# Intermediate rows in DRAM 256 bytes further apart, and stores of z in two transfers by partition halves

## The chip, the core and the metric

The kernel runs on one core of one Trainium2 chip. The metric is the device time of one execution in microseconds, the median over runs. A core has TensorE (matrix products, results in PSUM), VectorE (DVE), ScalarE (ACT), GpSimd (POOL) and SyncE (SP), which here issues nearly all transfers between DRAM and the on-chip memory SBUF. SBUF has 128 partitions. 16 DMA engines carry out the transfers.

## The reference, cut to what matters

Two parts follow each other: a causal convolution over the whole sequence by FFT (8 batches, 5696 tokens, 128 channels), and a soft mixture of experts on the 45568 tokens that come out of it.

```python
L = 2 * S
Xf = np.fft.rfft(x, n=L, axis=1)
Hf = np.fft.rfft(h, n=L, axis=0)
y = np.fft.irfft(Xf * Hf[None, :, :], n=L, axis=1)[:, :S, :]
...
logits = x @ phi                      # x is now y, (45568, 128)
d = softmax over tokens of logits; slot_input = d.T @ x
slot_out = expert MLPs (relu) of slot_input
c = softmax over slots of logits
return c @ slot_out
```

(The lines of the second part are shortened here to what they compute.) All data are float32, and the change touches only how two intermediate results of the convolution lie in DRAM.

## The kernel before, in words

The transform of 2 x 5696 points is split into N1 = 90 by N2 = 64, so that each stage is a set of small matrix products. NP = 45 is half of N1, HP = 64 half of the 128 partitions, D = 128 the channels.

**Stage A** (stage_a, line 205) takes one chunk of four columns (CH = 4) of one batch, folded by GpSimd (L201), multiplies it with a table (L212), lets ScalarE copy the result to the tile fst (L214), and stores it in DRAM as the spectrum f of that batch (L218). Each store of f moves 45 partitions, four packets of 1 KB each; there are two for each call, one from partitions 6 to 50 and one from 82 to 126. Eight steps make a batch, with two calls a step. Batch 0 is the filter h.

**Stage B** works in units u: a batch has 12 units, one or two a step. load_g (line 230) loads for a unit 128 rows of 4 KB of f into the tile gt (L236; three buffers, two units ahead). stage_b1 multiplies (L250) and VectorE applies the filter's spectrum (L268, L277). stage_b2 (line 281) transforms back (L292), ScalarE copies to the tile zst (L297), and one transfer stores it in DRAM as z (L300): 128 partitions, up to four packets of 1 KB each.

**Stage C** works in pairs of chunks. load_pair (line 320) loads 90 rows of 16 KB of z into the tile zc in two transfers (L328), 64 rows to partitions 32 to 95 and 26 rows to partitions 0 to 25 (z_blocks). stage_c1 makes the convolution's output from it (L347), and the further C stages make logits, both softmaxes and the slots' inputs. After the last step a tail runs the experts and writes the output (L817 to L828).

The order is written out by hand in one loop over steps t (line 561), with stage A of batch g + 1, stage B of batch g and stage C of an earlier batch side by side. A load of zc needs rows of z from all 12 units of its batch, so the first load of each batch waits for that batch's last store. SyncE issues the transfers strictly in the order of the program. The tile framework gives the transfers eight completion semaphores in turn, and a transfer waits until the last one on its semaphore, the eighth before it, has landed, beside the waits for its own data and buffers.

The two DRAM tensors of the change are declared on lines 126 and 127. A row of f is 45 x 2 x 128 floats, 46080 bytes. z has for each of 45 q a block of 128 rows of 1 KB, 131072 bytes, and a load of zc reads it as 90 half blocks, 65536 bytes apart.

Of the kernel before, what the change touches and what calls it, by code (L numbers as in the profile page):

```python
# [10 lines left out]
F32 = mybir.dt.float32  # L11
# [6 lines left out]
def z_blocks(n):  # L18

    return [(0, 64, 32), (64, n - 64, 0)]  # L20
# [54 lines left out]
def kernel(  # L75
# [24 lines left out]
    nc = tc.nc  # L100
    P = 128
    B, S, D = x.shape
# [4 lines left out]
    N1, N2 = 90, 64  # L107
    R1, HALF, NP = S // N2, N2 // 2, N1 // 2
    CH = 4
# [6 lines left out]
    HP = P // 2  # L116
# [6 lines left out]
    t_s1, t_i1, t_w, t_v, t_turn = [  # L123
        nc.inline_tensor(t, f"tab_{n}").ap()
        for n, t in zip(("s1", "i1", "w", "v", "turn"), transform_tables(S, N1, N2, CH, X0, F0, F1))]
    fd = [nc.dram_tensor(f"f_{g}", (2, N2, NP, 2, D), F32, kind="Internal").ap() for g in range(B + 1)]
    zd = [nc.dram_tensor(f"z_{b}", (NP, 2 * N2, 2, D), F32, kind="Internal").ap() for b in range(B)]
    cd = nc.dram_tensor("c_t", (P, B * NQ, Q, 2, MH), F32, kind="Internal").ap()

    const = ctx.enter_context(tc.tile_pool(name="const", bufs=1))  # L130
# [37 lines left out]
    def bank():  # L168
        rings.append(rings.pop(0))
        return rings[-1].tile([P, 512], F32, name="bank", tag="bank")  # L170
# [34 lines left out]
    def stage_a(c, comp):  # L205
        g, j = divmod(c, NJ)
        src = folded.pop((c, comp))
        tab = (0, 1) if comp == 0 else (1, 2)
        st = apool.tile([P, CH, 2, D], F32, name="fst", tag="fst", bufs=5)
        for G in range(2):  # L210
            p = bank()
            nc.tensor.matmul(p[:, :], s1[:, tab[G], :],  # L212
                             src[:, :, :].rearrange("p n d -> p (n d)"), start=True, stop=True)
            nc.scalar.activation(st[:, :, G, :],  # L214
                                 p[:, :].rearrange("p (n d) -> p n d", d=D), AF.Copy)
        n0 = comp * HALF + CH * j
        for a, p in enumerate((F0, F1)):
            nc.sync.dma_start(  # L218
                out=fd[g][a, n0:n0 + CH, :, :, :].rearrange("n q c d -> q n (c d)"),
                in_=st[p:p + NP, :, :, :].rearrange("k n c d -> k n (c d)"))  # L220


# [2 lines left out]
    def parts(u):  # L225

        g, w = divmod(u, NW)
        return g, w, [(i, min(2, NP - 2 * i)) for i in range(2 * w, min(2 * w + 2, NU))]

    def load_g(u):  # L230
        if u >= (B + 1) * NW:
            return
        g, w, us = parts(u)
        n = sum(k for _, k in us)
        t_ = bpool.tile([P, 4, 2, D], F32, name="gt", tag="gt", bufs=3)
        nc.sync.dma_start(  # L236
            out=t_[:, 0:n, :, :].rearrange("p q c d -> p (q c d)"),
            in_=fd[g].rearrange("a r q c d -> (a r) (q c d)")[:, 8 * w * D:(8 * w + 2 * n) * D])
        gs[u] = t_

    def stage_b1(u, share):
# [39 lines left out]
    def stage_b2(u):  # L281
        g, w, us = parts(u)
        if g == 0:
            return
        m = len(us)
        y_ = prods.pop(u)
        bz = bps.tile([P, 2, 2, 2 * D], F32, name="bz", tag="bz")
        for o, (i, n) in enumerate(us):
            for q in range(n):
                r = slice(q * HP, (q + 1) * HP)  # L290
                for a in range(2):
                    nc.tensor.matmul(bz[a * HP:(a + 1) * HP, q, o, :], vt[r, i, a, :],  # L292
                                     y_[r, a * m + o, :, :].rearrange("p c d -> p (c d)"),
                                     start=True, stop=True)
        n = us[0][1]
        st = bpool.tile([P, 2, 2, 2 * D], F32, name="zst", tag="zst", bufs=3)
        nc.scalar.activation(st[:, 0:m, 0:n, :].rearrange("p o q x -> p q o x"),  # L297
                             bz[:, 0:n, 0:m, :], AF.Copy)
        k = m * n
        nc.sync.dma_start(  # L300
            out=zd[g - 1][4 * w:4 * w + k, :, :, :].rearrange("q r c d -> r q (c d)"),
            in_=st[:, :, :, :].rearrange("p o q x -> p (o q) x")[:, 0:k, :])

# [14 lines left out]
    def load_pair(T):  # L320
        if T >= NT:
            return
        b, j = divmod(T, NQ)
        t_ = zring.pop(0)
        zring.append(t_)
        w_ = 2 * 2 * CH * 2 * D
        for r, n, p in z_blocks(N1):
            nc.sync.dma_start(  # L328
                out=t_[p:p + n, :, :, :, :, :].rearrange("k h o n c d -> k (h o n c d)"),
                in_=zd[b].rearrange("q (a r) c d -> (q a) (r c d)",  # L330
                                    a=2)[r:r + n, j * w_:(j + 1) * w_])
        zs[T] = t_

    def stage_c1(T, between):
# [226 lines left out]
    for t in range(last_front + 1):  # L561
# [6 lines left out]
        def prefetch(last):  # L568
            nonlocal loaded
            while loaded < len(queue) and queue[loaded][0] <= last \  # L570
                    and queue[loaded][0] // NW * NJ + NJ <= t:
                load_g(queue[loaded][0])
                loaded += 1
# [3 lines left out]
        def slot_b(place=None):  # L577
            if place is not None and place not in turns:
                return
            fresh = bool(us)  # L580
            if fresh:
                u = us.pop(0)
                prefetch(u + AHEAD)
                stage_b1(u, t < LAG_C or t >= NA)
                wait_b2.append(u)
            if len(wait_b2) > fresh:
                stage_b2(wait_b2.pop(0))

        if t < NA:
            stage_a(t, 0)  # L590
            fold(t + 1, 0)
# [30 lines left out]
        if pair(-2) is not None:  # L622
            load_pair(pair(-2))
# [6 lines left out]
        if t < NA:  # L630
            stage_a(t, 1)
            fold(t + 1, 1)
# [11 lines left out]
        if NA < t <= NA + E:  # L644
# [13 lines left out]
                      in_=zring[0][gap, :, :, :, :, :].rearrange("k h o n c d -> k (h o n c d)"))  # L658
    zring.insert(0, zn)
    load_pair(V + 2)  # L660
    nc.sync.dma_start(out=w1s[:, E - 1, :], in_=moe_w1[E - 1])
    tail["cT"] = last.tile([P, B, R1, 2 * NJ], F32, name="cT")
# [10 lines left out]
    for q in range(Q):  # L673
        r = slice(q * NSL, (q + 1) * NSL)
        nc.gpsimd.tensor_copy(out=rep4[r, :, :],
                              in_=ident[r, r].unsqueeze(1).broadcast_to([NSL, Q, NSL]))
    load_pair(T + 2)
    landed = []

# [14 lines left out]
    for V in range(T, NT):  # L694
# [30 lines left out]
        else:  # L725
            for i in range(4 * (V - T - 1), min(4 * (V - T), E), 2):
                nc.sync.dma_start(
                    out=w2s[:, i:i + 2, :, :],
                    in_=moe_w2[i:i + 2].rearrange("e (p c) d -> p e c d", p=P))
# [6 lines left out]
    p = bank()  # L736
# [8 lines left out]
    p = bank()  # L745
# [12 lines left out]
    for g in range(EG):  # L758
        for f0 in range(0, F, FH):
            p = bank()  # L760
# [10 lines left out]
    for g in range(EG):  # L771
        for k0 in range(0, NFC, 4):
            p = bank()
            for k in range(4):
# [3 lines left out]
                out=hidT[:, g, k0:k0 + 4, :], in_=p[:, :].rearrange("p (k c) -> p k c", k=4))  # L778
# [9 lines left out]
    p = bank()  # L788
# [18 lines left out]
    for b in range(B):  # L807
        for w0 in range(0, NV, G4):
            n = min(G4, NV - w0)
# [10 lines left out]
            for q in range(Q):  # L820
# [8 lines left out]
                out=ov[b, t0:t0 + n * RW * N2, :].rearrange("(w p n) d -> p w (n d)", p=P, n=CH),  # L829
                in_=o_[:, 0:n, :, :].rearrange("p w q d -> p w (q d)"))  # L830
            if lone:
                nc.sync.dma_start(
                    out=ov[:, NV * RW * N2:, :].rearrange("b (j n) d -> b j (n d)", n=CH),
                    in_=o_[:, n, :, :].rearrange("p q d -> p (q d)"))
# [29 lines left out]
```

## Time and profile before

The time is 920.01 us, the median of three runs (918.54 to 926.59). The profiled run's span is 914.5 us.

| What | Value |
|---|---|
| VectorE busy | 645.8 us (71%) |
| ScalarE busy | 481.1 us (53%) |
| GpSimd busy | 405.2 us (44%) |
| Read from DRAM, written to it | 142.86 MB, 128.21 MB |
| Stores of f (L218) | 288 of 180 KB |
| Loads of gt (L236) | 99 of 512 KB, 9 of 128 KB |
| Stores of z (L300) | 88 of 512 KB, 8 of 128 KB |
| Loads of zc and its twin zd (L328) | 32 of 1024 KB, 32 of 416 KB |
| Granted TensorE clock | 0.945 in the mean |

"Busy" is the time in which an engine has an instruction running; the DMA share is the time of all packets over 16 engines' span. The chain is followed back from the last instruction, at each step to what released it, so its shares say on what the end depended. A wait is written as "who line <- by what": total us, how often, the longest. Mean values over the span hide that the stages differ: the loop fills up until about 190 us, runs evenly until 673 us, and then empties into the tail.

### The profile page before, as it was taken

How to read it: one execution, taken by the hardware profiler on the slowest of the kernel's cores; microseconds unless marked ns; L12 is line 12 of the kernel's file. 1: busy time of each engine (PE TensorE's matmuls, PEld its weight loads, DVE VectorE, ACT ScalarE, POOL GpSimd, SP SyncE). 2: the span in 40 equal slices, each digit the busy share in tenths (PEclk: the TensorE clock that was granted, in tenths of full speed). 3: DMA queues.
4: the chain of work that ended last, by engine and by line, in shares of the span. 5: the costliest groups of instructions: out<-in, count | busy, mean ns of one | idle time of the engine just before them, and what ended most of it. 6: DMA issues, size and time to landing. Idle time of an engine off the chain costs nothing.

```text
span 914.5 us, 19226 instructions
## 1 busy us (share of the span) xinstructions
PE 812.2 (89%) x7220; PEld 425.9 (47%) x7220; DVE 645.8 (71%) x928; ACT 481.1 (53%) x888; POOL 405.2 (44%) x385
## 2 busy tenths in 40 slices
PE   6968888799999999999999999999988776978893
PEld 2323344344454444544555445444444443345783
DVE  3058767667888878877888777868888885774552
ACT  4624445456556565655666565555654344474442
POOL 4624333245555555555555555555533432472000
PEclk9989999999999999999999999999999998788865
DMA  9999899999999999999999999989989998751798
GB/s 302 269 282 310 256 326 347 292 323 340 285 324 331 304 281 323 320 329 280 329 323 317 289 317 313 311 281 325 334 266 338 305 295 206 223 220 74 281 404 340
DMA packets 156550, 272.43 MB, mean 298 GB/s; under 512 B 11766, under 2 KB 114422, under 8 KB 153317
## 3 DMA queue, kind: packets, MB, share of 16 engines
q1 hardware_dynamic: 155883, 270.85, 91.7%
q8 instruction: 58, 0.95, 0.4%
q10 hardware_dynamic: 576, 0.36, 0.2%
q14 instruction: 33, 0.27, 0.1%
HBM read 142.86 MB, written 128.21 MB: 296 GB/s over the span
## 4 chain that ended last, share of the span: by engine, by line
PE 61%; DMA 27%; issue 4%; ACT 2%; DVE 2%; POOL 2%; SPq 1%; DVEq 0%; POOLq 0%; ACTq 0%
PE bank L212 19%; PE bank L347 10%; PE bt L250 9%; DMA zc<-z 8%; PE bz L292 7%; DMA gt<-f 6%; DMA out_dram<-o 4%; PE bank L375 3%; PE bank L460 3%; DMA zd<-z 3%; DMA z<-zst 2%; DMA f<-fst 2%; PE bank L384 2%; PE bank L436 2%; PE op L817 1%
## 5 line engine op out<-in xcount | busy, mean ns | idle before, releaser
L201 POOL TENSOR_TENSOR x<-xc 128x512 f32<-128x512 f32 x144 | 183.1, 1273 | 260.5 <-PE bank L212 156.9
L212 PE MATMUL bank<-x,s 128*128 128x512 f32 x576 | 273.9, 611 | 9.7 <-POOL x L201 9.6
L214 ACT ACTIVATE fst<-bank 128x512 f32<-128x512 f32 x288 | 171.8, 597 | 94.7 <-PE bank L212 88.3
L297 ACT ACTIVATE zst<-bz 128x1024 f32<-128x1024 f32 x96 | 93.2, 971 | 195.2 <-PE bz L292 191.5
L268 DVE TENSOR_TENSOR p<-bt,Hi 128x1024 f32<-128x1024 f32 x96 | 113.0, 1177 | 107.3 <-PE bt L250 107.1
L212 PEld LDWEIGHTS bank<-x,s 128*128 128x128 f32 x576 | 102.1, 192 | 126.9 <-issue 94.1
L250 PE MATMUL bt<-gt,wt 64*64 64x256 f32 x1620 | 117.4, 397 | 40.0 <-DMA gt<-f 19.8
L347 PE MATMUL bank<-zc,i 128*64 128x512 f32 x480 | 118.0, 614 | 8.5 <-DMA zc<-z 6.2
L277 DVE TENSOR_TENSOR yf<-bt,p 128x512 f32<-128x512 f32 x192 | 119.4, 663 | 3.3
L268 DVE TENSOR_TENSOR bt<-bt,Hr 128x1024 f32<-128x1024 f32 x96 | 113.0, 1178 | 0.0
L250 PEld LDWEIGHTS bt<-gt,wt 64*64 64x64 f32 x1620 | 55.9, 134 | 117.0 <-issue 61.7
L292 PE MATMUL bz<-yf,vt 64*64 64x256 f32 x1440 | 103.7, 386 | 0.0
L366 POOL TENSOR_TENSOR y<-y,op 128x512 f32<-128x512 f32 x64 | 77.4, 1209 | 11.8 <-DVE op L352 9.1
L292 PEld LDWEIGHTS bz<-yf,vt 64*64 64x64 f32 x1440 | 61.8, 136 | 21.1
L366 POOL TENSOR_TENSOR y<-y,om 128x512 f32<-128x512 f32 x54 | 64.0, 1185 | 2.1
L347 PEld LDWEIGHTS bank<-zc,i 128*64 128x64 f32 x480 | 30.9, 138 | 70.3 <-issue 47.4
L375 PE MATMUL bank<-ident,y 109*128 109x109 f32 x512 | 57.5, 268 | 0.7 <-DVE y L366 0.7
L375 PEld LDWEIGHTS bank<-ident,y 109*128 109x128 f32 x512 | 51.2, 146 | 12.9 <-POOL L L449 6.2
L421 POOL MEMSET dt<- 64x8 f32 x32 | 3.4, 106 | 115.9 <-issue 69.2
L377 ACT ACTIVATE yt<-bank 128x360 f32<-128x360 f32 x128 | 50.2, 483 | 2.1 <-PE bank L375 2.1
L817 PE MATMUL op<-so,cT 32*128 32x128 f32 x704 | 46.2, 369 | 4.3 <-ACT o L826 3.4
L268 DVE TENSOR_TENSOR p<-bt,turn 128x1024 f32<-128x1024 f32 (+1 forms) x12 | 14.1, 1176 | 50.7 <-PE bt L250 50.6
(97 smaller groups left out, 861.5 us busy)
## 6 DMA issues: line engine op xcount, KB each, us to landing
f<-fst SPq DMA_DIRECT2D x288, 180.0 KB
gt<-f SPq DMA_DIRECT2D x99, 512.0 KB
z<-zst SPq DMA_DIRECT2D x88, 512.0 KB
zc<-z SPq DMA_DIRECT2D x30, 1024.0 KB
xc<-in_x_dram SPq DMA_DIRECT2D x64, 320.0 KB
out_dram<-o SPq DMA_DIRECT2D x16, 1024.0 KB
zc<-z SPq DMA_DIRECT2D x30, 416.0 KB
out_dram<-o SPq DMA_DIRECT2D x8, 768.0 KB
```

What stands on the lines that cost most here:

```text
L201: nc.gpsimd.tensor_tensor(out=y_[:, :, :], in0=t_[:, 0, :, :], in1=t_[:, 1, ::-1, :], op=AL.subtract if comp else AL.add)
L212: nc.tensor.matmul(p[:, :], s1[:, tab[G], :], src[:, :, :].rearrange("p n d -> p (n d)"), start=True, stop=True)
L214: nc.scalar.activation(st[:, :, G, :], p[:, :].rearrange("p (n d) -> p n d", d=D), AF.Copy)
L250: nc.tensor.matmul(bt[q * HP:(q + 1) * HP, a, o, :], wt[r, 2 * i + q, :], t_[r, 2 * o + q, :, :].rearrange("p c d -> p (c d)"), start=True ...
L268: nc.vector.tensor_tensor(out=p_, in0=pv, in1=h_, op=AL.mult)
L277: eng.tensor_tensor(out=y_[r, 0:k, c, :], in0=pv[:, :, c, :], in1=pi[r, 0:k, 1 - c, :], op=op_)
L292: nc.tensor.matmul(bz[a * HP:(a + 1) * HP, q, o, :], vt[r, i, a, :], y_[r, a * m + o, :, :].rearrange("p c d -> p (c d)"), start=True, sto ...
L297: nc.scalar.activation(st[:, 0:m, 0:n, :].rearrange("p o q x -> p q o x"), bz[:, 0:n, 0:m, :], AF.Copy)
L347: nc.tensor.matmul(p[h_ * HP:(h_ + 1) * HP, :], i1[0:kr, tab, :], t_[0:kr, h_, o, :, q, :], start=True, stop=True)
L366: eng.tensor_tensor(out=part_, in0=part(v, 0), in1=o_[:, :, :], op=sign)
L375: nc.tensor.transpose(p[:, i * TR:(i + 1) * TR], ys[T][0:TR, k * CH + i, 0:D], ident[0:TR, 0:TR])
L817: nc.tensor.matmul(pq[q][:, k * D:(k + 1) * D], cT[rows, b, r0:r0 + RW, :] if k < n else cL[rows, :, :], so4[rows, :], start=True, stop=True)
```

## The change

Both tensors get FILL = 64 floats, 256 bytes, at the end of each row: f behind each of its 128 rows of 46080 bytes, z behind each half block of 65536 bytes. The aim is that rows read side by side do not start at addresses a large round number apart. Since a half block of z is no longer followed directly by the next one, the 128 partitions of a z store can't be written by one regular pattern any more, and the store becomes two, one for each half of the partitions. The loads keep their shapes.

```diff
+    FILL = D // 2
-    fd = [nc.dram_tensor(f"f_{g}", (2, N2, NP, 2, D), F32, kind="Internal").ap() for g in range(B + 1)]
-    zd = [nc.dram_tensor(f"z_{b}", (NP, 2 * N2, 2, D), F32, kind="Internal").ap() for b in range(B)]
+    fd = [nc.dram_tensor(f"f_{g}", (2, N2, NP * 2 * D + FILL), F32, kind="Internal").ap() for g in range(B + 1)]
+    zd = [nc.dram_tensor(f"z_{b}", (NP, 2, N2 * 2 * D + FILL), F32, kind="Internal").ap() for b in range(B)]
...
-                out=fd[g][a, n0:n0 + CH, :, :, :].rearrange("n q c d -> q n (c d)"),
+                out=fd[g][a, n0:n0 + CH, 0:NP * 2 * D].rearrange("n (q x) -> q n x", x=2 * D),
...
-            in_=fd[g].rearrange("a r q c d -> (a r) (q c d)")[:, 8 * w * D:(8 * w + 2 * n) * D])
+            in_=fd[g].rearrange("a r x -> (a r) x")[:, 8 * w * D:(8 * w + 2 * n) * D])
...
-        nc.sync.dma_start(
-            out=zd[g - 1][4 * w:4 * w + k, :, :, :].rearrange("q r c d -> r q (c d)"),
-            in_=st[:, :, :, :].rearrange("p o q x -> p (o q) x")[:, 0:k, :])
+        for a in range(2):
+            nc.sync.dma_start(
+                out=zd[g - 1][4 * w:4 * w + k, a, 0:N2 * 2 * D].rearrange("q (r x) -> r q x", x=2 * D),
+                in_=st[a * HP:(a + 1) * HP, :, :, :].rearrange("p o q x -> p (o q) x")[:, 0:k, :])
...
-                in_=zd[b].rearrange("q (a r) c d -> (q a) (r c d)",
-                                    a=2)[r:r + n, j * w_:(j + 1) * w_])
+                in_=zd[b].rearrange("q a x -> (q a) x")[r:r + n, j * w_:(j + 1) * w_])
```

## The prediction

> **What bounds the kernel now.** I read the page first (busy shares, slices, chain), then a table by stage, then the chain around one change of batch, then the waits of the queue that issues the transfers, and last the packets of the trace by size.
>
> ```profile
> PE 812.2 (89%) x7220; PEld 425.9 (47%) x7220; DVE 645.8 (71%) x928; ACT 481.1 (53%) x888; POOL 405.2 (44%) x385
> ...
> DMA packets 156550, 272.43 MB, mean 298 GB/s; under 512 B 11766, under 2 KB 114422, under 8 KB 153317
> q1 hardware_dynamic: 155883, 270.85, 91.7%
> PE 61%; DMA 27%; issue 4%; ACT 2%; DVE 2%; POOL 2%; SPq 1%; DVEq 0%; POOLq 0%; ACTq 0%
> ```
>
> TensorE and the 16 DMA engines are both near full, and one queue, SyncE's, carries nearly all bytes. The page's average hides the stages:
>
> ```profile
> core 0: us, PE busy (x) PEld busy (x) DVE busy (x) ACT busy (x) POOL busy (x), PEclk, DMA share, GB/s
> 112.00:190.00 78.00, 66.13 (x515) 31.77 (x514) 52.73 (x62) 36.81 (x54) 24.98 (x20) 0.98 0.99 320
> 190.00:673.00 483.00, 472.66 (x4202) 237.21 (x4204) 385.12 (x549) 289.01 (x527) 261.79 (x243) 1.00 0.98 313
> 673.00:800.00 127.00, 100.73 (x974) 53.34 (x968) 97.75 (x155) 56.12 (x114) 45.00 (x50) 0.89 0.87 267
> 50.00:112.00 62.00, 51.90 (x301) 21.99 (x302) 46.62 (x53) 21.75 (x37) 22.85 (x18) 0.93 0.92 289
> ```
>
> Stores of z start at 112.8 us. From 112 to 190 us DMA alone is full (0.99). From 190 to 673 us, more than half of the span, both are: TensorE 472.66 of 483, DMA 0.98. How much lies between? The chain gives, where it stays on TensorE for a whole pair of steps, 21.1 us (244.1 to 265.2 us) to 21.6 us (265.2 to 286.8 us), and the mean pair from 200.5 to 660.7 us (21 pairs, by the starts of L212's matmuls) is 21.91 us. So TensorE's own work is some 21.4 us, and the DMA engines' 0.984 x 21.91 = 21.6 us. The difference to 21.91, about 0.5 us a pair or 11 us in this stage, is lost mostly where a batch ends:
>
> ```profile
> 298.23 12.96 DMA zc<-z
> ...
> 343.18 0.02 issue
> 343.20 0.12 ACT fst L214
> 343.32 5.75 DMA z<-zst
> 349.07 0.02 issue
> 349.08 0.03 SPq L328
> 349.11 0.04 issue
> 349.15 6.28 DMA zc<-z
> ```
>
> The first load of zc of a batch reads every row of its z, waits for the last store of z, and TensorE waits for it.
>
> ```profile
> SPq L236 <- DMA zc<-z: 51.8, 15, 4.7
> SPq L236 <- DMA f<-fst: 30.1, 5, 8.3
> SPq L300 <- DMA zc<-z: 23.3, 16, 2.3
> ```
>
> These are waits of the issuing queue from 190 to 673 us. The queue's transfers use eight semaphores in turn, each 96 or 97 times, so a transfer is issued only when the eighth before it has landed. Queued bytes, not the queue's speed, hold it up.
>
> Are the packets slow because of DRAM? I took the trace's packets from 190 to 673 us by size, in ns:
>
> ```
> bytes  what              count   median  mean
> 1024   stores of f, z    65457   46      48.3
> 4096   loads of gt        8346   159     201
> 16384  loads of zc        2026   620     840
> ```
>
> 4096 bytes in 159 ns and 16384 in 611 (the lowest tenth) are 25.8 and 26.8 bytes per ns and engine; nine stores in ten take 46 ns. In the load of zc from 258 to 263 us nearly all the first 64 packets took 611 ns, and the later ones some 900 to 1300: these are the 26 rows that go to partitions 0 to 25. The few slow gt packets (300 to 1500 ns) stand mostly at the head of a load, or beside the end of a zc load. So rows that lie 64 KB apart already load at one flat rate.
>
> [...]
>
> **The change part by part.**
> - *Bytes, shapes, arithmetic.* All packets keep size and number (45 x 4 x 1 KB, 128 x 4 KB, 64 x 16 KB); no engine's instruction changes except SyncE's. Nothing.
> - *Wider pitch* (f 46080 to 46336 bytes, a half row of z 65536 to 65792). Upper bound of the gain: all excess over the floor. For gt (201 - 159) x 8346 / 16 = 22 us of DMA time from 190 to 673 us; for stores (48.3 - 46) x 65457 / 16 = 9 us; for zc (840 - 611) x 2026 / 16 = 29 us, of which 26/90 x 2026 x 640 / 16 = 23 us (doubled packets, some 1250 ns)[...]. So at most 37 of 475 us, if every slow packet were DRAM's doing.[...] Rows now start on 256 instead of 1024 bytes; no run shows what that costs. I take 0 (ends: -37 and some +5 us).
> - *One more issue for each of the 96 stores.* Line 300 issues in 0.388 us (median), so 37 us more of SyncE's time over 645 us; SyncE is 1% of the chain, and what hides it is the wait for landings above. Where a batch ends, the second half's issue stands between the last zst and the load of zc: 8 x 0.39 = 3 us at most; I take 1.5. Behind it on the queue stand the stores of f and load_x, fed three steps ahead.
> - *Completion packets.* Each transfer leaves up to 16 of 4 bytes, 10.2 ns each: 96 x 16 x 10.2 / 16 = 1.0 us of DMA time.
> - *Half the partitions at a time.* 46080 packets of z, so each ns of mean is 2.9 us of DMA time. The nearest row is the stores of f, which already are two transfers of 45 partitions, each within one half. Alone on the queue (50 to 112 us) these take 52.2 ns in the mean, p90 71; mixed with others (190 to 673 us) f and z together take 48.3; z alone in whole stores (673 to 740 us, no f left) 48.5. So in the mixture halves cost no more than whole stores. I take 1 ns, 2.9 us; ends 0 and 3.9 ns (52.2 - 48.3), 11 us.
> - *Eight transfers in flight.* A pair of steps has 21 transfers with 6.8 MB (0.313 x 21.9), then 24. Eight of them hold 2.6 MB, 8.3 us at 313 GB/s; then 2.3 MB, 7.2 us. A wait of SyncE on compute longer than that drains the engines. From 190 to 673 us the waits on compute listed are at most 1.6 us, so one us less covers nothing new: 1 us; upper end 7 (share from 0.984 to 0.97).
>
> Sum: 1.0 + 2.9 = 3.9 us of DMA time. From 112 to 190 us it counts in full, where TensorE is as full by half: about 2.3 us. With 1.5 for the ends of batches and 1 for the shorter queue, some 4 to 5 us; less about 1.5 us for a small part of the excess that the pitch may remove: +3 us on 920, **923 us**.
>
> **The rivals.**
> - *No measurable difference (forecast, 0.53).* 911 to 929 us. For it: packets at their floor; halves of f cost nothing beside other work; TensorE full besides.
> - *The pitch removes DRAM conflicts (0.21).* For it: means are 26% (gt) and 35% (zc) above medians, and DMA is full in every stage from 112 us. Against: the slow packets' places, the flat floor. Half of the 37 us would be 18 of DMA time; TensorE's floor lets the middle stage gain at most 11, the ramp from 50 to 190 us some 4, the end 2. About 905 us.
> - *Halves and the shorter queue cost (0.26).* For it: the f-only packets (p90 71 against 46 ns)[...], and the middle stage has no slack in DMA. Against: the mixed mean. 11 us of DMA time, 7 of drained queue, 3 at ends of batches, four fifths of it counted: about +17, 937 us. With all stores at 73 ns it would be 46080 x 27 / 16 = 78 us, the far end, which f's own packets speak against.
>
> **How the numbers follow.** The range takes in the first rival's 905 and the second's 937 with a little beyond: 903 to 940 us leaves out some 2 in 10 with the far tails. Faster by over 1% (below 911): 0.21; slower by over 1% (above 929): 0.26; the rest 0.53.
>
> **What would show it.** Right: medians stay 46, 159 and 611 to 620 ns; the mean of the 1024-byte packets from 190 to 673 us between 48 and 50; mean pair between 21.8 and 22.1 us. Wrong towards faster: means of 4096- and 16384-byte packets well down, or 26-row loads faster. Wrong towards slower: 1024-byte packets around 73 ns, DMA share under 0.97 from 190 to 673 us, or longer chain pieces on z and zc where batches end.

## The result and the profile after

The changed kernel takes 988.56 us (median of four runs, 986.96 to 996.66) against 921.78 us before: a ratio of 1.074, with a 95% interval from 1.066 to 1.082. The forecast was 923 us and a range up to 940. The profiled run's span is 985.4 us. Medians in us are over all runs; ratios and intervals leave out the slow runs, those more than 1.5% above the fastest of their kernel.

The page of the changed kernel, the lines that answer to those of before:

```profile
PE 831.3 (84%) x7220; PEld 431.8 (44%) x7220; DVE 642.6 (65%) x928; ACT 481.0 (49%) x888; POOL 406.1 (41%) x385
...
DMA packets 158087, 272.44 MB, mean 276 GB/s; under 512 B 13302, under 2 KB 115958, under 8 KB 154853
...
q1 hardware_dynamic: 157419, 270.85, 88.6%
...
PE 45%; DMA 44%; SPq 3%; issue 3%; DVE 2%; ACT 2%; POOL 1%; DVEq 0%; ACTq 0%; POOLq 0%
DMA zc<-z 24%; PE bank L213 14%; PE bank L348 12%; DMA gt<-f 8%; PE bt L251 7%; DMA out_dram<-o 4%; PE bz L293 3%; DMA z<-zst 2%; DMA f<-fst 2%; PE bank L461 2%; PE bank L414 2%; PE bank L437 1%; SPq L219 1%; SPq L330 1%; DMA zd<-z 1%
```

The bytes are the same, 270.85 MB on SyncE's queue, and its 1536 more packets are the completions of 96 more transfers, 16 for each. The chain has gone from 61% TensorE and 27% DMA to 45% and 44%. Note that the DMA share *fell*, from 91.7% to 88.6%. 88.6% of 985.4 us is still 873 us of DMA time, where 91.7% of 914.5 us was 839: the DMA engines are busy for longer with the same bytes (+34 us), and stand still more often as well.

By stage (columns as before: us, then busy us of each engine, clock, DMA share, GB/s):

```profile
112.00:190.00 78.00, 64.78 (x501) 31.76 (x500) 49.06 (x57) 35.43 (x52) 24.14 (x19) 0.95 0.94 288
190.00:673.00 483.00, 438.82 (x3760) 218.28 (x3760) 344.49 (x494) 261.53 (x475) 236.13 (x217) 0.98 0.94 284
```

In the same 483 us TensorE got 438.82 us of work where it had 472.66, and the rate fell from 313 to 284 GB/s. What TensorE waits for is shown by the tile zc, the loads of z, first before and then after:

```profile
  DMA zc<-z: 6.2, 7
```

```profile
  DMA zc<-z: 48.1, 22
```

Seven waits of 6.2 us in all have become 22 with 48.1 us. The chain of the changed kernel from 296 to 350 us shows that it is no longer only at the change of a batch:

```profile
299.34 10.80 DMA zc<-z
...
323.70 10.22 DMA zc<-z
...
346.87 10.27 DMA zc<-z
```

Three pairs in a row, some 24 us apart, wait for their load. Before, one such wait at 298 us was followed by a pair without.

The packets of the trace from 190 to 673 us, in ns:

```
bytes   mean before   mean after   median before, after
1024       48.3          51.6          46, 46
4096      201           212           159, 159
16384     840           874           620, 702
```

The median has not moved for the two smaller sizes; what has grown is the share of long packets. Of the 1024-byte packets 4.2 in 100 took over 60 ns before, 11.0 after. Over the whole span the 1024-byte packets took 302.5 us of DMA time before and 320.3 after, all other sizes together some 17 us more.

The 1024-byte packets are f's and z's together. Those of z can be read apart from f's after the last store of f. There (from 8 us after the last issue of f to 8 us after the last of z: 681 to 766 us before, 740 to 833 us after) their mean rose from 48.6 to 52.2 ns, and the share over 60 ns from 4.8 to 14.7 in 100.

### The profile page after: what moved, and what is told of

Same layout as the page of the kernel before. It is cut to its first block, busy times and chain, and to the rows that moved or that the text cites. A ratio compares the mean times of both kernels' runs of the same rounds, so it can differ in the third digit from the quotient of the medians.

```text
span 985.4 us, 19335 instructions
## 1 busy us (share of the span) xinstructions
PE 831.3 (84%) x7220; PEld 431.8 (44%) x7220; DVE 642.6 (65%) x928; ACT 481.0 (49%) x888; POOL 406.1 (41%) x385
## 3 DMA queue, kind: packets, MB, share of 16 engines
q1 hardware_dynamic: 157419, 270.85, 88.6%
## 4 chain that ended last, share of the span: by engine, by line
PE 45%; DMA 44%; SPq 3%; issue 3%; DVE 2%; ACT 2%; POOL 1%; DVEq 0%; ACTq 0%; POOLq 0%
DMA zc<-z 24%; PE bank L213 14%; PE bank L348 12%; DMA gt<-f 8%; PE bt L251 7%; DMA out_dram<-o 4%; PE bz L293 3%; DMA z<-zst 2%; DMA f<-fst 2%; PE bank L461 2%; PE bank L414 2%; PE bank L437 1%; SPq L219 1%; SPq L330 1%; DMA zd<-z 1%
## 5 line engine op out<-in xcount | busy, mean ns | idle before, releaser
L213 PE MATMUL bank<-x,s 128*128 128x512 f32 x576 | 280.6, 624 | 8.9 <-DMA xc<-in_h_dram 8.0
L348 PE MATMUL bank<-zc,i 128*64 128x512 f32 x480 | 130.2, 667 | 49.7 <-DMA zc<-z 48.1
L213 PEld LDWEIGHTS bank<-x,s 128*128 128x128 f32 x576 | 104.6, 197 | 131.1 <-issue 99.9
L293 PE MATMUL bz<-yf,vt 64*64 64x256 f32 x1440 | 101.6, 378 | 0.0
L348 PEld LDWEIGHTS bank<-zc,i 128*64 128x64 f32 x480 | 34.2, 148 | 115.9 <-issue 95.8
L353 DVE TENSOR_TENSOR y<-bank,y 128x512 f32<-128x512 f32 x32 | 22.1, 691 | 64.5 <-PE bank L348 64.3
L357 ACT ACTIVATE y<-bank 128x512 f32<-128x512 f32 x32 | 19.1, 598 | 77.2 <-PE bank L348 77.2
L376 PE MATMUL bank<-ident,y 109*128 109x109 f32 x512 | 56.1, 264 | 0.7 <-DVE y L367 0.7
```

The costliest lines, as they stand in the source:

```text
L213: nc.tensor.matmul(p[:, :], s1[:, tab[G], :], src[:, :, :].rearrange("p n d -> p (n d)"), start=True, stop=True)
L348: nc.tensor.matmul(p[h_ * HP:(h_ + 1) * HP, :], i1[0:kr, tab, :], t_[0:kr, h_, o, :, q, :], start=True, stop=True)
L376: nc.tensor.transpose(p[:, i * TR:(i + 1) * TR], ys[T][0:TR, k * CH + i, 0:D], ident[0:TR, 0:TR])
```

## The experiments

The loss can sit in the second transfer as such (theory A), in the halves (theory B) or in the pitch (theory C). The first four kernels take the change apart. Each ratio is to the kernel before, with its 95% interval.

**The pitch of f alone.** Edits of the declaration, the store and the load of f as in the change; z as before.

```diff
-    fd = [... (2, N2, NP, 2, D) ...]
+    fd = [... (2, N2, NP * 2 * D + FILL) ...]
```

> Only the rows of f lie 256 bytes further apart; z and its stores stay as before. Theory A (two transfers for each store of z take too much of SyncE's issue time) and theory B[...]: no change, 915 to 928 us. Theory C (rows that start on 256 instead of 1024 bytes make transfers slower): slower by about half of what the change lost, 945 to 965 us, and it would show already between 50 and 112 us, before any store of z, where the changed kernel needed 117 us to come as far as the kernel before did in 112.

Measured: 928.15 us, ratio 1.003 (0.999 to 1.007). Its 1024-byte packets from 200 to 650 us have a mean of 48.1 ns, before 48.4. The pitch of f costs nothing. The slow start from 50 to 112 us does appear here, with a DMA share of 0.86 and a granted clock of 0.86. But the last two kernels of this section, which leave f as it was and store no z before 117 us, show a clock of 0.86 and a share of 0.89 there, so the pitch is not needed for it.

**The halves alone.** No row moves.

```diff
-        nc.sync.dma_start(
-            out=zd[g - 1][4 * w:4 * w + k, :, :, :].rearrange("q r c d -> r q (c d)"),
-            in_=st[:, :, :, :].rearrange("p o q x -> p (o q) x")[:, 0:k, :])
+        for a in range(2):
+            r = slice(a * HP, (a + 1) * HP)
+            nc.sync.dma_start(
+                out=zd[g - 1][4 * w:4 * w + k, r, :, :].rearrange("q r c d -> r q (c d)"),
+                in_=st[r, :, :, :].rearrange("p o q x -> p (o q) x")[:, 0:k, :])
```

> Only the stores of z become two transfers by partition halves; no row moves. Theory A: nearly all of the loss, 975 to 995 us, line of the store on SyncE with about 0.6 us for each issue, DMA share from 200 to 650 us near 0.94. Theory B: the same time, but then the 1024-byte packets of z carry it: their mean between 51 and 53 ns. Theory C: no change, 915 to 930 us.

Measured: 990.28 us, ratio 1.072 (1.066 to 1.078). This is the whole loss. The mean of the 1024-byte packets from 200 to 650 us, a stretch that all the following figures of this kind use, is 51.6 ns, with 10.8 in 100 over 60 ns, as in the changed kernel (51.6 and 10.9).

**Two transfers by rows q.** The same packets and bytes, but each transfer with all 128 partitions. The eight stores of a single row stay whole, so there are 184 transfers and not the 192 of the halves.

```diff
+        for q0 in range(0, k, 2):
+            q1 = min(q0 + 2, k)
+            nc.sync.dma_start(
+                out=zd[g - 1][4 * w + q0:4 * w + q1, :, :, :]...,
+                in_=st...[:, q0:q1, :])
```

> The stores of z become two transfers as well, but each takes all 128 partitions and half of the packets of each (two of four rows q); no row moves. Number of transfers, bytes and packets are those of the halves. Theory A: as slow as the halves, 975 to 995 us. Theory B: [...]about the time of the kernel before plus a few us, 920 to 935 us.

Measured: 937.47 us, ratio 1.015 (1.010 to 1.019), mean packet 48.7 ns. Theory A, which asked for 975 us and more, falls: 88 more transfers cost 1.5%, about a fifth of the loss. The stage from 190 to 673 us of the halves, and then of this kernel:

```profile
190.00:673.00 483.00, 433.22 (x3728) 216.20 (x3732) 335.37 (x486) 257.23 (x469) 235.77 (x217) 0.98 0.94 281
```

```profile
190.00:673.00 483.00, 461.44 (x4016) 231.41 (x4012) 366.32 (x528) 277.98 (x506) 253.82 (x235) 0.99 0.97 300
```

281 against 300 GB/s. What differs is the choice of partitions, and with it the shape: 64 partitions by four packets against 128 by two.

**The pitch of z alone, stores whole.** The fill stands behind each block of 128 rows, so that one regular pattern still covers a store; a load of zc reads its rows as pairs of half blocks.

```diff
-    zd = [... (NP, 2 * N2, 2, D) ...]
+    zd = [... (NP, 2 * N2 * 2 * D + FILL) ...]
```

> Only z's blocks of 128 rows lie 256 bytes further apart (131328 instead of 131072 bytes), and the stores stay whole, one transfer of 128 partitions; a load of zc reads its rows in pairs of half blocks. Theories A and B: no change, 915 to 930 us. Theory C: slower by about half of the loss, 945 to 965 us, with longer packets of 1024 and 16384 bytes.

Measured: 929.27 us, ratio 1.001 (0.997 to 1.004). Theory C falls for z as well. The fill lies between blocks here, not between half blocks; for those, the changed kernel (988.56) and the halves without a pitch (990.28) are alike.

So it is the halves. What about them: which partitions a transfer reads (theory P), or the shape of 64 partitions (theory S)? No trace here shows by what means the choice of partitions would act; what theory P expects of each kernel below is the author's estimate. For theory S spoke that SyncE's issues of z had become longer. The stores of z in SyncE's rows, duration in ns (least / median / most), for the kernel before and the one after:

```profile
L300 SPq DMA_DIRECT2D z<-zst x96: 320/388/1155, 112.8 to 758.0; - x96
```

```profile
L302 SPq DMA_DIRECT2D z<-zst x192: 468/608/1710, 118.0 to 825.2; - x192
```

**Both transfers from partitions 32 to 95**, and **both from 0 to 63**: the shape of the halves, other partitions. The partitions not named are left out, so what is stored is not z; the work is the same.

```diff
-                in_=st[r, :, :, :]...
+                in_=st[32:96, :, :, :]...      # the other kernel: st[0:64, ...]
```

> As the halves without a wider pitch (990 us), same two issues, same shape of 64 partitions by four packets, same places in DRAM, but both transfers read partitions 32 to 95 of the tile[...]; what is stored is thereby in part the wrong rows of z (partitions 0 to 31 and 96 to 127 are left out). Theory P[...]: about the time of the two transfers by rows q, 930 to 945 us, issues of z on SyncE back from 0.61 to some 0.45 us, mean of the 1024-byte packets back below 49.5 ns. Theory S (the shape of 64 partitions itself takes longer to issue): as slow as the halves, 980 to 1000 us, issues near 0.61 us.

Measured: 942.24 us, ratio 1.016 (1.007 to 1.025), mean packet 48.4 ns, much as with two transfers by q. Its stage from 190 to 673 us, and its issues of z:

```profile
190.00:673.00 483.00, 461.31 (x4072) 231.42 (x4069) 373.74 (x533) 278.90 (x508) 256.22 (x237) 1.00 0.97 303
```

```profile
L302 SPq DMA_DIRECT2D z<-zst x192: 535/605/1916, 114.7 to 777.8; - x192
```

One part of the expectation missed: the issues are as long as in the halves, 605 ns. So the shape does lengthen the issue, but that costs no time that shows beyond the 1.5% of two transfers. Theory S explains the issue and not the time.

> As the halves, but both transfers read partitions 0 to 63 (partitions 64 to 127 are left out, so half of the stored rows are the wrong ones).[...] Theory P: slower than the halves, 1000 to 1040 us, with more 1024-byte packets over 60 ns than the 11 in 100 of the halves. Theory S: the same as the halves, 980 to 1000 us.

Measured: 1002.68 us in one run and 1019 to 1021 us in three, so without a ratio or an interval; its profile is not read here. All four are above the halves' 990, as theory P has it for two transfers from the same half. On its own this run shows little; the single transfer from the same partitions, below, has an interval.

**Two transfers of 48 and 80 partitions.**

```diff
+        for r in (slice(0, 48), slice(48, P)):
```

> The stores of z as two transfers by partitions 0 to 47 and 48 to 127, no wider pitch, output complete.[...] Theory P:[...] 940 to 975 us. Theory S (it is the 64 partitions[...]): as two transfers by rows q, 930 to 945 us.

Measured: 967.07 us, ratio 1.041 (1.034 to 1.048), mean packet 50.4 ns and 7.4 in 100 over 60 ns. In the time and in the share over 60 ns it lies between whole partitions (ratio 1.015, 4.6 in 100) and halves (1.072, 10.8 in 100), as theory P expects. After the last store of f, where z's packets stand alone, it does not: their mean is 54.0 ns there, above the 52.2 of the changed kernel.

**A load of zc split at 80 rows** instead of 64, stores as before.

```diff
-    return [(0, 64, 32), (64, n - 64, 0)]
+    return [(0, 80, 32), (80, n - 80, 0)]
```

> The stores as before. The load of zc is split at 80 rows to partitions 32 to 111 and 10 rows to partitions 0 to 9, in place of 64 to 32 to 95 and 26 to 0 to 25. In the kernel before the 26 rows took doubled packets, 23 us of DMA time from 190 to 673 us. [...] (theory P), most of the doubling goes, mean of the 16384-byte packets from 840 to under 750 ns, and the time falls by 3 to 12 us, since TensorE is nearly full beside it. [...]no change, 918 to 930 us.

Measured: 961.55 us, ratio 1.032 (1.025 to 1.040): the wrong way. The mean of the 16384-byte packets from 200 to 650 us rose from 838 to 1061 ns and their median from 622 to 1108, although only 10 rows instead of 26 went to partitions from 0 on. So the larger transfer, whose 64 rows lay clean at 611 ns, came to be slow itself; why is not shown. What the run does show is that how a load is split over partitions moves its packets by a quarter, with no transfer more. Of the two outcomes expected, the faster one was theory P's and the unchanged time its contrary; neither came, so why the 26 rows are slow in the kernel before is not settled. Its stage from 190 to 673 us has a DMA share of 1.00 at 296 GB/s.

**One transfer for each store, all from half the partitions.** Left to ask was whether the choice of partitions alone also empties the engines, or whether the doubled issues and the eight transfers in flight do that. These two kernels have no transfer more than the kernel before; they too leave out half the partitions and do not store z.

```diff
+        v = st[0:64, 0, 0, 0:1]                # the control: st[32:96, ...]
+        v = bass.AP(tensor=v.tensor, offset=v.offset,
+                    ap=[v.ap[0], [D // 2 if k > 1 else 0, 2 * k], [1, 2 * D]])
         nc.sync.dma_start(
-            out=zd[g - 1][4 * w:4 * w + k, :, :, :].rearrange("q r c d -> r q (c d)"),
-            in_=st...[:, 0:k, :])
+            out=zd[g - 1][4 * w:4 * w + k, :, :, :].rearrange("q (a r) c d -> r (q a) (c d)", a=2),
+            in_=v)
```

> One transfer for each store of z, as in the kernel before, with the same 512 packets to the same places in DRAM, but all read from partitions 0 to 63 (eight packets from each, overlapping pieces of the row; partitions 64 to 127 are left out, so what is stored is not z). No second issue, no shorter row of eight transfers. [...]985 to 1020 us, as with two transfers from partitions 0 to 63, and the DMA share from 190 to 673 us below 0.95. If half of the loss comes from the doubled issues and the queue of eight: 945 to 965 us with the share near 0.98.

Measured: 1005.29 us, ratio 1.087 (1.077 to 1.097); mean packet 56.1 ns, 17.9 in 100 over 60 ns.

> The control of it: one transfer, eight packets from each of 64 partitions, overlapping pieces as well, but from partitions 32 to 95 (the other partitions are left out). [...]the time of the kernel before, 918 to 935 us, 1024-byte packets at 48 to 49 ns in the mean. If 64 partitions with eight packets each, or the overlapping reads, are slow as such: as slow as the same from partitions 0 to 63.

Measured: 936.0 us beside 926.83 us of the kernel before on the same chip, ratio 1.001 (0.998 to 1.005), or 1.010 by the medians of all runs, so the shape costs at most some 1%; mean packet 48.3 ns, 4.3 in 100 over 60 ns. The stage from 190 to 673 us, first from partitions 0 to 63, then from 32 to 95:

```profile
190.00:673.00 483.00, 426.08 (x3641) 212.92 (x3634) 332.67 (x480) 252.60 (x458) 230.48 (x213) 0.98 0.94 276
```

```profile
190.00:673.00 483.00, 463.20 (x4108) 234.13 (x4112) 375.19 (x534) 282.65 (x515) 258.38 (x238) 1.00 0.98 307
```

The two kernels differ in one number, the first partition of a source, and by 8.6% in time (7.4% by the medians of all runs). The one from partitions 0 to 63 has both marks of the changed kernel, the long packets and the DMA share of 0.94, with no issue added. After the last store of f, its z packets take 62.3 ns in the mean, those of the control 48.3. No version beat the kernel before.

## Why the prediction was wrong

- **Bounds.** Right: from 190 us on, DMA and TensorE were both full (0.98 and 472.66 of 483 us until 673 us). The conclusion that about 4 us of DMA time would partly hide was not tested by its own size, since that size was wrong.
- **The pitch: 0.** Right, though the sum then takes off 1.5 us for it after all. Both pitches alone give 1.003 and 1.001, within a few tenths of a per cent of nothing. The flat 611 ns of the loads were the right line to read. At pitches of 45 and 64 KB the runs show no loss to remove. The ceiling of 37 us was 22 + 9 + 29 less the 23 of the 26-row packets; that these could not be the pitch's doing was the author's estimate. The rival that the pitch removes DRAM conflicts had nothing to gain.
- **One more issue, completions, eight in flight: 1.5 + 1.0 + 1 us.** Too small by a factor of four: two transfers by q, with eight fewer added transfers, cost 1.48%, some 14 us on 924. The signs were right.
- **Half the partitions at a time: 1 ns, at most 3.9 ns (11 us). This is the step that failed.** Against 320.3 - 302.5 = 18 us of DMA time for all 1024-byte packets, it had 2.9. If all of that is z's, it is 17.8 us x 16 / 46080, or 6.2 ns for each packet of z, above the upper end. A fair price for z's packets by themselves was in hand: f's stores before any z took 52.2 ns, and z's own halves after the last f took 52.2 as well, 3.6 more than whole stores. The prediction let it go because f and z mixed (48.3 ns) were no slower than z alone (48.5), so that halves should cost nothing beside other work. With z in halves the mixture rose to 51.6. So the mixed mean before said nothing on halves of z. Why f's stores, which also lie within one half each, do not show in that mean stays open. That they are 45 partitions and not 64 is not a sufficient reason: 48 and 80 partitions still cost 4%. Which 64 partitions a store reads does count: after the last store of f, z's packets took 62.3 ns from partitions 0 to 63 and 48.3 from 32 to 95. In which way is not shown; the trace does not name a packet's engine or its partition. The 73 ns end, 78 us, had been worked out and then set aside on the evidence of f (in the kernel before, until 50 us, a tenth of f's packets took 73 ns or more).
- **What was not priced at all: idle engines.** Idle time was priced only for the queue of eight, 1 us and at most 7. At least 16 packets of SyncE's queue were under way in 67% of the time from 215 to 650 us before, in 50% after. The prediction turned DMA time into kernel time at four fifths at most; here 34 us of DMA time came with 67 us. The single transfer from partitions 0 to 63 (51% of the time, from 32 to 95 66%) shows that the idle time comes with the choice of partitions and needs no further issue. In which way stays open. Issues on SyncE do become longer with it: those of the same 772 transfers take 586.9 us in all with the stores from partitions 0 to 63 and 479.7 with them from 32 to 95. No run tells cause from effect here. A single row is a poor witness of it: the store of c_t, which no kernel here touches, takes 327 ns to issue before and 896 after, but nearly the same with the stores from partitions 0 to 63 (546 ns) and with them from 32 to 95 (533). Its rows before, after, and in those from partitions 0 to 63 and 32 to 95:

```profile
L495 SPq DMA_DIRECT2D c_t<-cst x25: 319/327/470, 246.0 to 758.5; - x25
```

```profile
L496 SPq DMA_DIRECT2D c_t<-cst x25: 335/896/1100, 264.2 to 826.6; - x25
```

```profile
L498 SPq DMA_DIRECT2D c_t<-cst x25: 329/546/585, 270.7 to 842.9; - x25
```

```profile
L498 SPq DMA_DIRECT2D c_t<-cst x25: 319/533/1539, 253.4 to 770.5; - x25
```

- **The other packets.** They took 17 us more DMA time after, which the prediction did not price beyond 1 us of completions. Only part of it can come from the choice of partitions: two transfers by q have 10 us of it too.
- **The signs of the prediction.** Of those named for "slower", two came true: longer pieces on zc, and a share of 0.94, under the 0.97 named. The third, 1024-byte packets around 73 ns, did not come in the mean (51.6 ns) or the median (46); 11 in 100 were over 60 ns. Of those named for "right", the mean between 48 and 50 ns failed.

## What to carry to other kernels

Where DMA is full (0.98 here), look at which partitions a transfer touches before its bytes: stores from partitions 0 to 63 alone, or from 0 to 63 and 64 to 127 in turn, cost 7 to 9% of this kernel, one from 32 to 95 with the same shape at most 1%. If a layout forces a split, split by rows across all partitions (1.5% here), not by halves. A row of the profile that looks like the new operation gives a price where it stands by itself; when the two ends of an unknown are 0 and 78 us, an average over mixed packets is not enough to drop the far end.

## What the runs showed of the hardware

- The first partition of a source made the difference: stores of 512 packets from partitions 0 to 63 gave 276 GB/s and from 32 to 95 gave 307, in the same kernel and stage.
- The medians hide it. The median of 1024-byte packets is 46 ns before and after the change; the share over 60 ns (4.3, 7.4, 10.8, 17.9 in 100) orders the ratios to the kernel before (1.001, 1.041, 1.072, 1.087).
- Stores from partitions 0 to 63 lower the DMA share instead of raising it: 0.94, against 0.98 from 32 to 95. A lower share was no free capacity (ratio 1.087). The slower loads of zc (1061 ns a packet in the mean) raised it, to 1.00.
- The length of an issue of z on SyncE differed with the shape of the transfer (64 partitions by four packets 0.605 us, 128 by two 0.455 us), and that difference did not show in the time (ratios 1.016 and 1.015).
